# Pooling attention and a token/channel mixer on one core: first batch pooled on TensorE, loads reordered, side work woven at half slots

## The chip, the cores and the metric

The kernel runs on one core of a Trainium2 chip. The metric is device time in microseconds (us), the median over several executions. A profile is one execution with the hardware profiler on. Its engines are PE (TensorE, matmuls; PEld is its load of weights), DVE (VectorE), ACT (ScalarE), POOL (GpSimd) and SP (SyncE, which here only starts transfers).

## The reference

Two parts follow each other. Attention has 8 batches, 8 heads, 576 tokens and 64 columns per head, with keys and values averaged over groups of 8 tokens; the mixer works on 576 x 512 per batch. All inputs and the output are float32.

```python
k_p = k.reshape(B, H, 72, 8, D).mean(axis=3)          # keys, and values likewise
attn = softmax(q @ k_p.T / sqrt(D))                    # 576 x 72 per head
x = (attn @ v_p), heads side by side                   # 576 x 512 per batch
h = relu(x.T @ w_tok1) @ w_tok2                        # over tokens, 256 wide
u = x + h.T
out = u + relu(u @ w_ch1) @ w_ch2                      # over channels, 1536 wide
```

## The kernel before

**Tiling.** The 576 tokens of a batch are split as 64 partitions x 9 rows. Two rows make a chunk of 128 tokens, so a batch has four full chunks and half a one left over; the halves of two batches share a tail chunk. The even rows (0, 2, 4, 6, 8) come first and the odd ones last (`ORDER`, line 41).

**A batch's attention and token mixing** (`batch_steps`, lines 140 to 274) is a list of steps:
- `prepare` (147) pools keys and values by additions (`pool8`, 127: three additions per half of the heads, lines 130, 131 and 133 or 136). Batch 0 is pooled on VectorE, the others on GpSimd (152).
- `kpT` (172) transposes the pooled keys on TensorE into one PSUM buffer `pt`, and VectorE copies them into `kTs` (180). `qT` (184) transposes the queries of a pair of heads into the same `pt` (189), and ScalarE copies them out (191). There is one `pt` buffer (line 57), so each use waits until the one before it was copied out.
- `score` (194) multiplies for two heads, and ScalarE takes the exponential (204).
- `av` (208) is the attention output of one chunk: eight matmuls (214), then VectorE divides (219, 222) into `x`, or `xt` for the half chunk.
- `at` (227), `u` (240) and `uT` (254) are the token mixer, the residual sum and its transpose.

**A unit** (`unit_steps`, 277) is the channel mixer of one batch: 12 groups `g(m)` of four matmuls with w_ch1 (287), each with a Relu on ScalarE or VectorE in turn (290, 292), then for each of four chunks 12 matmuls with w_ch2 in three parts (300), an addition on VectorE (305) and two stores by SP (308). Units 0 to 7 are the batches, unit 8 is the four tail chunks.

**Order of the work.** TensorE and GpSimd run in the order in which the code is written (line 315); VectorE's and ScalarE's order is chosen by the framework's scheduler. The start-up issues all loads on GpSimd's queue: keys, queries and values of batch 0, w_tok1, w_ch1, w_ch2, then batch 1 (lines 316 to 323); w_tok2 goes over SP's queue as float32 (97). At most eight of GpSimd's transfers are under way, and the next waits for the oldest. Batch 0's steps run alone. Then, in unit n, the steps of batch n + 1 are woven between the 24 pieces of the unit, from piece 14 to 26 in unit 0 and from 0 to 22 later, evenly by their number (lines 336 to 343); GpSimd starts the loads of batch n + 2 (333) and pools batch n + 1.

Of the kernel before, what the change touches and what calls it, by code (L numbers as in the profile page):

```python
# [13 lines left out]
POOLE = mybir.EngineType.Pool  # L14


@with_exitstack
def kernel(
# [22 lines left out]
    ORDER = list(range(0, BR, 2)) + list(range(1, BR, 2))  # L41
# [23 lines left out]
    f2 = singles.tile([P, 2, S], FP32)  # L65
# [7 lines left out]
    def load(b):  # L73
        if b >= B:
            return
        kr = raw.tile([SP, H, POOL, D], BF16, name="kr")
        vr = raw.tile([SP, H, POOL, D], BF16, name="vr")
        qb = raw.tile([P, HP * BR * D + D], BF16, name="qb")
        nc.vector.memset(qb[:, HP * BR * D:], 0.0)  # L79
        loaded[b] = (kr, vr, qb)  # L80
        parts = 2 if b == 0 else 1

        def kv(t, src, g):
            n = H // parts
            nc.gpsimd.dma_start(out=t[:, g * n:(g + 1) * n].rearrange("j h i d -> j h (i d)"),  # L85
                                in_=src[b, g * n:(g + 1) * n].rearrange("h (j i) d -> j h (i d)", i=POOL))
        for g in range(parts):
            kv(kr, k, g)
            n = HP // parts
            nc.gpsimd.dma_start(  # L90
                out=qb[:, g * n * BR * D:(g + 1) * n * BR * D].rearrange("p (a e) -> p a e", a=n),
                in_=q[b, 2 * g * n:2 * (g + 1) * n].rearrange("(a l) (p r) d -> (l p) a (r d)", l=2, r=BR))
# [25 lines left out]
    def load_ch():  # L118
# [21 lines left out]
    def batch_steps(b):  # L140
# [6 lines left out]
        def prepare():  # L147
# [24 lines left out]
        def kpT(h0, h1):  # L172
            def go():
# [90 lines left out]
        if first:  # L264
            steps = [kpT(0, HP), qT(0), score(0, 0), score(0, 1), qT(1), score(1, 0), score(1, 1),
                     kpT(HP, H), qT(2), score(2, 0), score(2, 1), qT(3), score(3, 0), score(3, 1)]
        else:
            steps = [kpT(0, H), qT(0), qT(1)]
            for hp in range(HP):
                steps += [score(hp, 0)] + ([qT(hp + 2)] if hp + 2 < HP else []) + [score(hp, 1)]  # L270
        steps += [av(c) for c in range(5)]
        steps += [at(0), at(1), u(0), u(1), uT(0), u(2), uT(1), u(3)]
        steps += ([u(4), uT(2), uT(4)] if par else [uT(2)]) + [uT(3)]
        return prepare, steps, st


    def unit_steps(n, st):
        w = {}

        def g(m):  # L280
            def go():
                if m == 0:
                    w["GT"] = gtp.tile([P, NM, 4 * P], BF16, name="GT")
                uT = uT_tails if n == B else st["uT"]
                ps = ps_one.tile([P, 512], FP32, name="p1")
                for kk in range(4):
                    nc.tensor.matmul(out=ps, lhsT=w_ch1[:, kk, m * P:(m + 1) * P], rhs=uT[:, kk, :],  # L287
                                     start=(kk == 0), stop=(kk == 3))
                if m % 2 == 0:
                    nc.scalar.activation(out=w["GT"][:, m, :], in_=ps, func=AF.Relu)  # L290
                else:
                    nc.vector.tensor_scalar(out=w["GT"][:, m, :], in0=ps, scalar1=0.0, scalar2=None, op0=ALU.max)  # L292
            return go

        def o(c, part):
            def go():
                if part == 0:
                    w["ps"] = ps_one.tile([P, 512], FP32, name="p1")
                for m in range(part * 4, part * 4 + 4):
                    nc.tensor.matmul(out=w["ps"], lhsT=w["GT"][:, m, c * P:(c + 1) * P], rhs=w_ch2[:, m, :],  # L300
                                     start=(m == 0), stop=(m == NM - 1))
                if part < 2:
                    return
                o_sb = outp.tile([P, DM], FP32, name="o")
                nc.vector.tensor_tensor(out=o_sb, in0=w["ps"], in1=(u_tails if n == B else st["u"])[:, c, :], op=ALU.add)
                for half in range(2):
                    b, r = (2 * c + half, ORDER[8]) if n == B else (n, ORDER[2 * c + half])
                    nc.sync.dma_start(out=out[b].rearrange("(p r) n -> p r n", r=BR)[:, r, :],
                                      in_=o_sb[half * BP:(half + 1) * BP, :])
            return go  # L310

# [3 lines left out]
    with tc.manual_schedule(engines={PE, POOLE}):  # L315
# [11 lines left out]
        for s in batches[0][1]:  # L327
            s()
# [45 lines left out]
```

## Time and profile before

| | us |
|---|---|
| median of 3 runs | 333.67 |
| lowest, highest | 332.85, 335.69 |
| profiled execution, its own time | 336.74 |
| span of the profiled execution | 335.0 |
| PE busy | 287.1 (86%) |
| DVE busy | 157.2 (47%) |
| POOL busy | 152.2 (45%) |
| ACT busy | 96.4 (29%) |

The span goes from the first to the last instruction; the profiled execution's own time is 1.74 us longer. Busy time counts an engine's instructions, and for a matmul its modelled end. The unit starts of the profiled execution, from its timeline, are 47.2, 89.6, 124.5, 157.8, 189.9, 223.2, 255.3, 288.5 and 309.3 us.

### The profile page before, as it was taken

The numbers are of one execution on the slowest core, as the hardware profiler recorded it, in microseconds if no ns is written. First come the engines' busy times: TensorE is split into PE (matmuls) and PEld (weight loads), VectorE is DVE, ScalarE is ACT, GpSimd is POOL, SyncE is SP. The second block draws the span as 40 slices with busy tenths as digits, with TensorE's granted clock in tenths as the row PEclk, the third lists the DMA queues.
The fourth block names the chain that finished last, engine by engine and source line by source line (L and its number), as shares of the span: only waits on it lengthen the run. The fifth ranks groups of instructions, "written<-read, shape, count | busy, mean of one in ns | idle before, by whom it ended". The sixth has DMA issues, their size and how long they took to land.

```text
span 335.0 us, 4535 instructions
## 1 busy us (share of the span) xinstructions
PE 287.1 (86%) x1840; PEld 149.9 (45%) x1840; DVE 157.2 (47%) x304; ACT 96.4 (29%) x161; POOL 152.2 (45%) x142
## 2 busy tenths in 40 slices
PE   0026879788699998999899899989998999999994
PEld 0024434453355455544554455445544554444441
DVE  3650554134624653665355526653655266433321
ACT  3026013250056007500750083008302820120300
POOL 7382398089608950994099329999200000000000
PEclk9999999797879999999999999999999999999998
DMA  7999993574327344815291628130022002204114
GB/s 131 184 162 201 204 198 43 101 112 94 58 45 112 62 71 97 135 39 92 73 142 33 104 65 140 38 82 7 0 63 64 2 0 64 65 0 95 33 31 94
DMA packets 26756, 27.95 MB, mean 83 GB/s; under 512 B 4848, under 2 KB 21872, under 8 KB 26736
## 3 DMA queue, kind: packets, MB, share of 16 engines
q0 software_dynamic: 20704, 17.64, 35.3%
q1 hardware_dynamic: 6032, 10.03, 11.9%
q8 instruction: 14, 0.23, 0.3%
q14 instruction: 6, 0.05, 0.0%
HBM read 35.85 MB, written 9.44 MB: 135 GB/s over the span
## 4 chain that ended last, share of the span: by engine, by line
PE 77%; DVE 14%; DMA 4%; ACT 2%; issue 2%; POOL 1%; DVEq 0%; POOLq 0%
DVE x L222 4%; DMA vr<-in_v_dram 4%; PE pt L189 4%; PE pt L260 3%; DVE GT L292 2%; DVE u L251 1%; ACT ex L204 1%; DVE kTs_92 L180 1%; DVE den L219 1%; DVE kTs_91 L180 1%; PE p_504 L300 1%; PE p_644 L300 1%; ACT qT L191 1%; DVE uT L261 1%; PE p_3181 L300 1%
## 5 line engine op out<-in xcount | busy, mean ns | idle before, releaser
L300 PEld LDWEIGHTS <-GT 128*128 128x128 bf16 x432 | 40.2, 98 | 40.6 <-issue 1.1
L287 PEld LDWEIGHTS <-w_ch_86 128*128 128x128 bf16 x432 | 41.3, 99 | 38.1 <-issue 2.4
L90 POOL DMA_DIRECT2D qb<-in_q_dram x9 | 6.9, 770 | 65.9 <-PE pt L189 42.9
L191 ACT COPY qT<-pt 128x640 bf16<-128x640 bf16 x32 | 22.1, 690 | 36.6 <-PE pt L189 36.6
L189 PE MATMUL pt<-ident,qb 128*128 128x128 bf16 x160 | 16.2, 239 | 15.6 <-DVE kTs_91 L180 10.1
L189 PEld LDWEIGHTS <-qb 128*128 128x128 bf16 x160 | 12.5, 108 | 21.7 <-issue 17.4
L214 PEld LDWEIGHTS <-ex 72*128 72x128 bf16 x320 | 14.5, 102 | 13.3 <-DVE x L222 7.5
L176 PE MATMUL pt<-ident,kp 72*128 72x72 bf16 x64 | 4.1, 211 | 15.2 <-DVE kp L133 15.2
L261 DVE COPY uT<-pt 128x512 bf16<-128x512 bf16 x32 | 13.4, 418 | 5.0 <-PE pt L260 5.0
L260 PEld LDWEIGHTS <-u 128*128 128x128 bf16 x128 | 9.6, 97 | 10.8 <-DVE u L251 2.7
L260 PE MATMUL pt<-ident,u 128*128 128x128 bf16 x128 | 12.4, 219 | 2.1 <-DVE uT L261 0.7
L231 PEld LDWEIGHTS <-w_tok_83 128*128 128x128 bf16 x80 | 8.5, 107 | 11.5 <-issue 4.1
L201 PEld LDWEIGHTS <-kTs_91 128*72 128x72 bf16 x64 | 8.1, 129 | 8.9 <-issue 4.3
L176 PEld LDWEIGHTS <-kp 72*128 72x128 bf16 x64 | 3.7, 108 | 17.2 <-DVE kp L133 15.2
L201 PEld LDWEIGHTS <-kTs_92 128*72 128x72 bf16 x64 | 7.2, 115 | 5.9 <-issue 1.0
L250 PEld LDWEIGHTS <-w_tok_84 128*128 128x128 bf16 x64 | 6.1, 99 | 7.2 <-issue 1.4
L85 POOL DMA_DIRECT2D kr<-in_k_dram x9 | 7.6, 842 | 0.9 <-POOLq L358 0.9
L180 DVE COPY kTs_91<-pt 64x576 bf16<-64x576 bf16 (+1 forms) x10 | 3.9, 389 | 8.5 <-PE pt L176 8.4
L85 POOL DMA_DIRECT2D vr<-in_v_dram x9 | 7.4, 819 | 0.4 <-issue 0.4
L79 DVE MEMSET qb<- 128x32 uint32 x8 | 0.7, 85 | 10.5 <-PE pt L189 9.7
L130 POOL TENSOR_TENSOR t_368<-kr 72x1024 f32<-72x1024 bf16 x1 | 2.1, 2113 | 6.0 <-DMA kr<-in_k_dram 6.0
L290 ACT ACTIVATE GT<-p_1495 128x512 bf16<-128x512 f32 x1 | 0.6, 597 | 14.0 <-PE p_1495 L287 14.0
(780 smaller groups left out, 680.0 us busy)
## 6 DMA issues: line engine op xcount, KB each, us to landing
out_dram<-o SPq DMA_DIRECT2D x72, 128.0 KB, 2.4
kr<-in_k_dram POOLq DMA_DIRECT2D x7, 576.0 KB, 8.1
qb<-in_q_dram POOLq DMA_DIRECT2D x7, 576.0 KB, 6.0
vr<-in_v_dram POOLq DMA_DIRECT2D x7, 576.0 KB, 9.7
w_ch_86<-in_moe_w_ch_dram POOLq DMA_DIRECT2D x3, 512.0 KB, 7.2
w_ch_87<-in_moe_w_ch_dram POOLq DMA_DIRECT2D x2, 768.0 KB, 13.8
f_88<-in_moe_w_tok_dram SPq DMA_DIRECT2D x1, 576.0 KB, 4.0
kr<-in_k_dram POOLq DMA_DIRECT2D x2, 288.0 KB, 8.2
```

Source lines behind the costliest of these rows:

```text
L85: nc.gpsimd.dma_start(out=t[:, g * n:(g + 1) * n].rearrange("j h i d -> j h (i d)"), in_=src[b, g * n:(g + 1) * n].rearrange("h (j i) d -> ...
L180: nc.vector.tensor_copy(out=kT[rows, half, h0 * SP:h1 * SP], in_=ps[rows, h0:h1, :].rearrange("p h j -> p (h j)"))
L189: nc.tensor.transpose(out=ps[:, rr].rearrange("m l p -> m (l p)"), in_=st["qb"][:, o:o + P], identity=ident)
L191: nc.scalar.copy(out=st["qT"][:, hp].rearrange("m l (r p) -> m r l p", p=BP), in_=ps)
L201: nc.tensor.matmul(out=ps[0:SP, hl, 0:n], lhsT=kT[:, odd, h * SP:(h + 1) * SP], rhs=st["qT"][:, hp, hl, 0:n], start=True, stop=True)
L214: nc.tensor.matmul(out=ps[:, h // 4, (h % 4) * (D + 1):(h % 4 + 1) * (D + 1)], lhsT=st["ex"][:, h * S + n0:h * S + n0 + P], rhs=st["vp"][: ...
L222: nc.vector.tensor_tensor(out=dst.rearrange("p (a h d) -> p a h d", a=2, d=D), in0=view[:, :, :, 0:D], in1=den[rows, :, :, None].broadcast ...
L231: nc.tensor.matmul(out=ps, lhsT=w_tok1[:, c if c < 4 else 4 + par, m * P:(m + 1) * P], rhs=st["x"][:, c, :] if c < 4 else st["xt"], start= ...
L260: nc.tensor.transpose(out=ps[:, kk, :], in_=src[:, kk * P:(kk + 1) * P], identity=ident)
L261: nc.vector.tensor_copy(out=dst[:, :, o:o + P], in_=ps)
L287: nc.tensor.matmul(out=ps, lhsT=w_ch1[:, kk, m * P:(m + 1) * P], rhs=uT[:, kk, :], start=(kk == 0), stop=(kk == 3))
L300: nc.tensor.matmul(out=w["ps"], lhsT=w["GT"][:, m, c * P:(c + 1) * P], rhs=w_ch2[:, m, :], start=(m == 0), stop=(m == NM - 1))
```

## The change

- **Batch 0 is pooled on TensorE.** `ppool` adds the eight tokens of a group by eight matmuls with the identity into one PSUM bank. Keys are then copied twice, by ScalarE and by VectorE; values once, by VectorE.
- **Loads.** The first two of four head pairs' queries of batch 0 go over SP's queue as float32 and are cast by ScalarE and VectorE; both halves of the keys go first on GpSimd's queue. w_tok2 is cast on its way in, over GpSimd's queue, and VectorE permutes it just ahead of batch 0's outputs. Batch 1 is loaded ahead of w_ch2, which comes in three parts.
- **Odd rows first** (`ORDER`), so that w_tok1 loads in four transfers.
- **Head order by hand**, on VectorE and ScalarE too. In the head VectorE copies the queries and ScalarE half of the keys.
- **Pooling later.** The first half of batches 1 and 2 is pooled on VectorE, the rest on GpSimd. Two small memsets per batch move from GpSimd to VectorE.
- **Weave.** A unit now gives way 48 times: after two matmuls of each g group and of each output chunk. Tables say after which half slot each step of the next batch stands.

In the names below kr, vr and qb are a batch's keys, values and queries as loaded, w_ch_86 and w_ch_87 are w_ch1 and w_ch2, f_88 is w_tok2 as loaded, w_tok_84 is w_tok2 permuted, kp is the pooled keys, pt the transpose buffer, and p_ a PSUM bank.

The first place is GpSimd's queue in the start-up, from w_ch1 to batch 1; before:

```order
L121 DMA w_ch_86<-in_moe_w_ch_dram 128x4x512 x3
L123 DMA w_ch_87<-in_moe_w_ch_dram 128x6x512 x2
L85 DMA kr<-in_k_dram 72x8x512
L90 DMA qb<-in_q_dram 128x4x576
L85 DMA vr<-in_v_dram 72x8x512
```

and after:

```order
L136 DMA w_ch_86<-in_moe_w_ch_dram 128x4x512 x3
L91 DMA kr<-in_k_dram 72x8x512
L95 DMA qb<-in_q_dram 128x4x576
L91 DMA vr<-in_v_dram 72x8x512
L140 DMA w_ch_87<-in_moe_w_ch_dram 128x4x512 x3
```

Batch 1's three transfers now stand ahead of w_ch2.

The second place is VectorE's queue at the first scores of batch 0, with what each instruction waits for; before:

```order
L131 TENSOR_TENSOR t_157<-t_157 72x4x128 [waits DVE_49]
L136 TENSOR_TENSOR vp<-t_153 72x4x64 [waits DVE_49]
L136 TENSOR_TENSOR vp<-t_157 72x4x64 [waits DVE_49]
L169 MEMSET xt 128x256 x2
L180 COPY kTs_91<-pt 64x288 [waits PE_49]
```

and after:

```order
L212 CAST kp<-p_151 72x4x64 [waits Activation_49]
L226 COPY qT<-pt 128x5x2x64 [waits PE_49]
L199 COPY kTs_92<-pt 64x288 [waits Activation_49]
L226 COPY qT<-pt 128x5x2x64 [waits PE_49]
L212 CAST kp<-p_199 72x4x64 [waits Activation_49]
```

The additions that pooled keys and values are gone; copies of pooled keys and of queries stand there, and the copies of pooled and of transposed keys wait for ScalarE's half of the same copy.

The third place is VectorE's queue at batch 0's attention outputs; before:

```order
L79 MEMSET qb 128x32
L219 RECIPROCAL den<-p_242 128x8
L222 TENSOR_TENSOR x<-p_242,den 128x512
L219 RECIPROCAL den<-p_254 128x8
L222 TENSOR_TENSOR x<-p_254,den 128x512
L219 RECIPROCAL den<-p_266 128x8
```

and after:

```order
L129 COPY w_tok_84<-f_88 128x320
L131 COPY w_tok2t<-w_tok_84 128x2x64 x2
L256 RECIPROCAL den<-p_273 128x8
L259 TENSOR_TENSOR x<-p_273,den 128x512
L256 RECIPROCAL den<-p_285 128x8
L259 TENSOR_TENSOR x<-p_285,den 128x512
L256 RECIPROCAL den<-p_297 128x8
L147 TENSOR_TENSOR t_400<-kr 72x1024
L259 TENSOR_TENSOR x<-p_297,den 128x512
L256 RECIPROCAL den<-p_309 128x8
L148 TENSOR_TENSOR t_400<-t_400 72x4x128
L259 TENSOR_TENSOR x<-p_309,den 128x512
```

The permutation of w_tok2 stands ahead of the first output, and batch 1's key additions (t_400) stand between the outputs.

The diff, cut to its core:

```diff
-    ORDER = list(range(0, BR, 2)) + list(range(1, BR, 2))
+    NO = BR - NE
+    ORDER = list(range(1, BR, 2)) + list(range(0, BR, 2))
+    CHUNK = [1, 3, 0, 2]
...
+        if b == 0:
+            for a in range(2):
+                nc.sync.dma_start(out=qf[:, a:a + 1, :], in_=q_in(a, a + 1))
+            kv(kr, k, 0, HP)
+            kv(kr, k, HP, H)
+            make_identity(nc, ident)
+            q_cast(2, HP)
+            kv(vr, v, 0, HP)
+            kv(vr, v, HP, H)
+            nc.scalar.copy(out=qb[:, 0:BR * D], in_=qf[:, 0, :])
+            nc.vector.tensor_copy(out=qb[:, BR * D:2 * BR * D], in_=qf[:, 1, :])
+        else:
+            kv(kr, k, 0, H)
+            q_cast(0, HP)
+            kv(vr, v, 0, H)
 
     def load_tok():
-        nc.sync.dma_start(out=f2, in_=moe_w_tok2.rearrange("(c p) n -> p c n", p=P))
+        nc.gpsimd.dma_start(out=f2, in_=moe_w_tok2.rearrange("(c p) n -> p c n", p=P))
...
+    def permute_tok2():
         src = f2.rearrange("t m (p r) -> t m r p", r=BR)
         dst = w_tok2.rearrange("t m (r p) -> t m r p", p=BP)
         for m in range(2):
-            nc.scalar.copy(out=dst[:, m, 0:NE], in_=src[:, m, 0:BR:2, :])
-            nc.vector.tensor_copy(out=dst[:, m, NE:BR], in_=src[:, m, 1:BR:2, :])
+            nc.vector.tensor_copy(out=dst[:, m, 0:NO], in_=src[:, m, 1:BR:2, :])
+            nc.vector.tensor_copy(out=dst[:, m, NO:BR], in_=src[:, m, 0:BR:2, :])
...
+            if not first:
+                engs = [nc.vector if b < 3 else nc.gpsimd, nc.gpsimd]
+                for g in range(2):
+                    hs = slice(g * HP, (g + 1) * HP)
+                    pool8(engs[g], kr, hs, kp[:, hs], True)
...
+                    copy = nc.scalar.copy if first and half == 0 else nc.vector.tensor_copy
+                    copy(out=kT[rows, half, h0 * SP:h1 * SP], in_=ps[rows, h0:h1, :].rearrange("p h j -> p (h j)"))
+        def ppool(t, g):
+            def go():
+                ps = ps_one.tile([P, 512], FP32, name="p1")
+                hs = slice(g * HP, (g + 1) * HP)
+                for i in range(POOL):
+                    nc.tensor.matmul(out=ps[0:SP, 0:HP * D], lhsT=ident[0:SP, 0:SP], rhs=st[t][:, hs, i, :],
+                                     start=(i == 0), stop=(i == POOL - 1))
+                view = ps[0:SP, 0:HP * D].rearrange("j (h d) -> j h d", d=D)
+                if t == "kr":
+                    nc.scalar.copy(out=st["kp"][:, hs, 0, :], in_=view)
+                    nc.vector.tensor_copy(out=st["kp"][:, hs, 1, :], in_=view)
+                else:
+                    nc.vector.tensor_copy(out=st["vp"][:, hs, 0:D], in_=view)
...
-                nc.scalar.copy(out=st["qT"][:, hp].rearrange("m l (r p) -> m r l p", p=BP), in_=ps)
+                dst = st["qT"][:, hp].rearrange("m l (r p) -> m r l p", p=BP)
+                if first:
+                    nc.vector.tensor_copy(out=dst, in_=ps)
+                else:
+                    nc.scalar.copy(out=dst, in_=ps)
...
+                nc.tensor.matmul(out=ps, lhsT=w_ch1[:, kk, m * P:(m + 1) * P], rhs=uT[:, kk, :],
+                                 start=(kk == 0), stop=(kk == 3))
+                if kk == 1:
+                    yield
...
+                if m % 2 == 1 and m < NM - 1:
+                    yield
...
+    HEAD = """kpool0 q0 kpT0 o0 e0 q1 o1 e1 kpool1 q2 kpT1 o2 e2 q3 o3 e3 vpool0 vpool1 av0 av1 av2 av3 av4
+              at0 at1 u0 u1 t0 u2 t1 u3 t2 t3"""
...
+    LATER = {0: "kpT", 2: "q0", 4: "q1", 5: "o0", 6: "q2", 7: "e0", 9: "o1", 10: "q3", 11: "e1", 13: "o2", 15: "e2",
...
+        with tc.manual_schedule(engines={DVE, ACT}):
+            load(0)
...
+            load_tok()
+            load_ch1()
+            load(1)
+            load_ch2()
+            batches[0][0]()
+            for s in HEAD.split():
+                if s == "av0":
+                    permute_tok2()
+                batches[0][1][s]()
         for n in range(B + 1):
...
+            for i, _ in enumerate(unit_steps(n, batches[n][2] if n < B else None)):
+                for s in at.get(i, "").split():
+                    if (n + 1) % 2 or s not in ("u4", "t4"):
+                        side[s]()
```

In `HEAD` and the tables o and e are a pair's scores of odd and even rows, q, t and u stand for `qT`, `uT` and `u`. In unit 0 the table `FIRST` begins with `kpT0` at half slot 14 and ends with `t3 t4` at 47; in `LATER` av0 stands at 22, at0 at 32, u0 at 36, and t4, which only odd batches have, at 47.

## Rows read from the trace of the kernel before

**Rows 1.** Units' stretches: length; PE, PEld, DVE, ACT, POOL busy; clock, DMA share, GB/s.
```profile
47.20:57.73 10.53, 10.53 (x49) 4.79 (x49) 3.46 (x5) 3.58 (x6) 10.14 (x9) 1.00 0.66 94
57.73:89.61 31.88, 25.50 (x174) 13.57 (x173) 14.21 (x30) 7.78 (x13) 20.03 (x18) 0.89 0.50 89
89.61:124.49 34.88, 33.58 (x215) 17.79 (x215) 15.98 (x31) 11.25 (x19) 19.95 (x17) 0.90 0.45 72
124.49:157.82 33.33, 32.03 (x223) 17.02 (x222) 17.82 (x35) 11.26 (x19) 19.97 (x17) 1.00 0.50 90
157.82:189.91 32.09, 30.79 (x215) 16.52 (x214) 16.67 (x32) 11.26 (x19) 19.96 (x17) 1.00 0.48 84
```

**Rows 2.** Waits of TensorE, 15 to 89, then 89 to 289 us: total, times, longest.
```profile
PE pt L176 <- DVE kp L133: 15.2, 1, 15.2
...
PE pt L189 <- DVE kTs_91 L180: 6.7, 2, 6.0
...
PE pt L189 <- DVE kTs_91 L180: 3.3, 3, 1.1
...
PE pt L189 <- DVE kTs_92 L180: 3.3, 3, 1.1
```

**Rows 3.** The same view in stretches of 2 us.
```profile
36.00:38.00 2.00, 1.78 (x18) 1.06 (x16) 1.93 (x5) 0.00 (x0) 0.00 (x0) 1.00 1.24 208
...
60.00:62.00 2.00, 0.58 (x10) 0.34 (x9) 1.51 (x3) 0.00 (x0) 0.00 (x0) 1.00 0.93 153
62.00:64.00 2.00, 1.20 (x11) 0.97 (x12) 0.00 (x0) 0.73 (x2) 0.00 (x0) 0.70 1.00 217
64.00:66.00 2.00, 2.00 (x7) 0.83 (x6) 0.00 (x0) 0.66 (x1) 0.00 (x0) 0.50 0.05 16
```

**Rows 4.** Timeline of the start-up, its chain: start, length, engine, line.
```profile
8.52 1.22 DVE L130 TENSOR_TENSOR t_145<-kr 72x1024 f32<-72x1024 bf16 x1 [2.61 <-DMA kr<-in_k_dram]
...
24.05 0.74 PE L189 MATMUL pt<-ident,qb 128*128 128x128 bf16 x5
...
24.94 0.69 ACT L191 COPY qT<-pt 128x640 bf16<-128x640 bf16 x1
...
26.41 0.70 ACT L204 ACTIVATE ex<-p_197 72x640 bf16<-72x640 f32 x1 [0.78 <-PE p_197 L201]
```

**Rows 5.** The same timeline, TensorE in at(0) and at(1), and GpSimd.
```profile
37.01 1.90 PE L231 MATMUL p_302<-x,w_tok_83 128*128 128x512 bf16 x4
...
39.05 2.11 POOL L130 TENSOR_TENSOR t_368<-kr 72x1024 f32<-72x1024 bf16 x1 [6.03 <-DMA kr<-in_k_dram]
...
39.12 1.91 PE L231 MATMUL p_309<-x,w_tok_83 128*128 128x512 bf16 x4
...
40.83 0.63 PE L231 MATMUL p_309<-xt,w_tok_83 128*128 128x512 bf16 x1
```

**Rows 6.** The same timeline, VectorE alone.
```profile
4.73 0.79 DVE L114 CAST w_tok_84<-f_88 128x256 bf16<-128x256 f32 x2 [1.68 <-DMA f_88<-in_moe_w_tok_dram]
...
5.55 0.32 DVE L116 COPY w_tok2t<-w_tok_84 128x128 bf16<-128x128 bf16 x2
...
13.29 0.68 DVE L131 TENSOR_TENSOR t_145<-t_145 72x512 f32<-72x512 f32 x1
...
14.49 0.68 DVE L133 TENSOR_TENSOR kp<-t_145 72x512 bf16<-72x512 f32 x1
...
20.07 0.42 DVE L136 TENSOR_TENSOR vp<-t_157 72x256 bf16<-72x256 f32 x1
...
27.07 0.62 DVE L180 COPY kTs_91<-pt 64x288 bf16<-64x288 bf16 x2 [5.56 <-PE pt L176]
...
36.67 0.69 DVE L222 TENSOR_TENSOR x<-p_278,den 128x512 bf16<-128x512 f32 x1
...
37.50 0.68 DVE L222 TENSOR_TENSOR xt<-p_290,den 64x512 bf16<-64x512 f32 x1
...
43.89 0.41 DVE L261 COPY uT<-pt 128x512 bf16<-128x512 bf16 x1
```

More of the change, by code (lines that the diff above doesn't have):

```diff
@@ L80, in load @@
         loaded[b] = (kr, vr, qb)
[L81 to L92, printed above, removed]
@@ L108, in load_tok @@
+        for half in range(2):
+            rows = slice(half * BP, (half + 1) * BP)
             nc.gpsimd.dma_start(out=w_tok1[rows, 4 + half, :], in_=w[:, ORDER[8], :])
-        nc.vector.memset(w_tok2t, 0.0)
+    def permute_tok2():
         src = f2.rearrange("t m (p r) -> t m r p", r=BR)
@@ L262, in uT @@
             return go
[L264 to L272, printed above, removed]
@@ L273, in batch_steps @@
-        steps += ([u(4), uT(2), uT(4)] if par else [uT(2)]) + [uT(3)]
-        return prepare, steps, st
-    def unit_steps(n, st):
[L278 to L310, printed above, removed]
-        return [g(m) for m in range(NM)] + [o(c, part) for c in range(4) for part in range(3)]
@@ L315 @@
[L315 to L328 removed]
+        name = {f"kpT{g}": kpT(g * HP, (g + 1) * HP) for g in range(2)}
+        name["kpT"] = kpT(0, H)
@@ new lines, in batch_steps @@
+        for g in range(2):
+            name[f"kpool{g}"], name[f"vpool{g}"] = ppool("kr", g), ppool("vr", g)
+        for hp in range(HP):
+            name[f"q{hp}"], name[f"o{hp}"], name[f"e{hp}"] = qT(hp), score(hp, 1), score(hp, 0)
+        for c in range(5):
+            name[f"av{c}"], name[f"u{c}"], name[f"t{c}"] = av(c), u(c), uT(c)
+        name["at0"], name["at1"] = at(0), at(1)
+        return prepare, name, st
+    def unit_steps(n, st):
+        GT = gtp.tile([P, NM, 4 * P], BF16, name="GT")
+        uT = uT_tails if n == B else st["uT"]
+        u_all = u_tails if n == B else st["u"]
+        for m in range(NM):
+            ps = ps_one.tile([P, 512], FP32, name="p1")
+            for kk in range(4):
+                nc.tensor.matmul(out=ps, lhsT=w_ch1[:, kk, m * P:(m + 1) * P], rhs=uT[:, kk, :],
+                                 start=(kk == 0), stop=(kk == 3))
+                if kk == 1:
+                    yield
+            if m % 2 == 0:
+                nc.scalar.activation(out=GT[:, m, :], in_=ps, func=AF.Relu)
+            else:
+                nc.vector.tensor_scalar(out=GT[:, m, :], in0=ps, scalar1=0.0, scalar2=None, op0=ALU.max)
+            yield
+        for c in range(4):
+            ps = ps_one.tile([P, 512], FP32, name="p1")
+            for m in range(NM):
+                nc.tensor.matmul(out=ps, lhsT=GT[:, m, c * P:(c + 1) * P], rhs=w_ch2[:, m, :],
+                                 start=(m == 0), stop=(m == NM - 1))
+                if m % 2 == 1 and m < NM - 1:
+                    yield
+            o_sb = outp.tile([P, DM], FP32, name="o")
+            nc.vector.tensor_tensor(out=o_sb, in0=ps, in1=u_all[:, c, :], op=ALU.add)
+            for half in range(2):
+                b, r = (2 * c + half, ORDER[8]) if n == B else (n, ORDER[2 * c + half])
+                nc.sync.dma_start(out=out[b].rearrange("(p r) n -> p r n", r=BR)[:, r, :],
+                                  in_=o_sb[half * BP:(half + 1) * BP, :])
+            yield
```

88 lines of the change are left out of this document (40 added, 48 removed).

## The prediction

> **What bounds the kernel now.** I read the share of busy time first, then the span cut at the starts of the stages, then the waits of TensorE, its clock in short stretches, and last the timeline of the start-up. TensorE is the bound in most of the span: in units 2 and 3 it is busy 32.03 of 33.33 us and 30.79 of 32.09 us, so a steady unit loses 1.30 us [rows 1]. The time to be had is elsewhere. Up to 47.2 us no unit has begun: TensorE first waits 15.2 us for VectorE's pooling of the keys, then 6.0 us for the copy into kTs, which stands behind the pooling of the values on VectorE [rows 2]. Unit 0 then takes 10.53 + 31.88 = 42.4 us, although its work is that of unit 2 (32.03 us): TensorE is idle 6.4 us of it, and the granted clock is 0.89 in its second part [rows 1]. In short stretches that is 0.50 in 64 to 66 us, the 1.2 GHz level, after a stretch at 60 to 62 us in which TensorE worked 0.58 of 2 us [rows 3]. Unit 1 takes 34.88 us at a clock of 0.90 where unit 3, with the same work, takes 32.09 [rows 1].
>
> **Head.** Edits: pooling of batch 0 by identity matmuls, half the queries over SP, VectorE's and ScalarE's order by hand. I follow the new chain in us of the span.
>
> The first half of the keys lands when it does now, as the same bytes go ahead of it on SP's queue (0.59 MB, w_tok2 or these queries): 8.5 [rows 4]. Each pooling is eight matmuls of 256 columns; four of 512 columns go in 39.12 to 40.83 us [rows 5], 0.43 each and so at the 1.2 GHz level, which makes 0.21 for 256 columns and 1.7 a pooling: 10.2. Its two copies out run one after the other, since the order makes VectorE's wait for ScalarE's. A copy of 72 x 256 is no row out of PSUM; VectorE's 72 x 256 out of SBUF took 0.42 [rows 6], and I take 0.4 each (bounds 0.3 and 0.7): 11.3. The copy of the queries, now on VectorE, must free the one transpose buffer before the keys' transposes: uT of 128 x 512 took 0.41 there [rows 6], so 0.5 for 640 columns against ScalarE's 0.69 [rows 4]: 11.9. Transposes 0.45, and two copies into kTs, also in series, 0.85 (two took 0.62 [rows 6], plus a hand-over): 13.2. Scores of a head pair (1152 columns at that rate) 0.96, transposes of the next queries 0.74 [rows 4], copy with hand-overs 0.7, scores 0.96: 16.6. The second half repeats this with its pooling in front (4.6 before the scores, 3.35 for them): 24.5. The two poolings of the values 3.4 and their copy 0.55: 28.5. Then, by the order, VectorE permutes w_tok2 before it may touch the first attention output: two of 128 x 256 took 0.79, two of 320 would take 0.96, and the two small copies 0.32 [rows 6]: 30.5.
>
> There the gain is mostly given back. Five outputs at 0.83 from one to the next [rows 6] are 4.2, and between them stand three additions for batch 1 (1.22 [rows 4], 0.68, 0.68 [rows 6]), 2.6 in all: the last output xt is ready at 37.3, where it now ends at 38.2 [rows 6]. One matmul of at0 and five of at1 follow (now the last begins at 40.83 [rows 5]); unit 0 begins 1.2 us earlier, at 46.0. VectorE stalls if batch 1's keys are not there at about 32.4. They land at 39.05 now [rows 5]; w_ch2, 1.5 MB that no longer goes before them, is 7.6 us at the 208 GB/s of [rows 3], so 31.5: just in time. If they came as late as now, xt would end near 44, 5.9 us later than before. Were the paired copies parallel and the value poolings at the high clock, it would be 2 us better.
>
> [...]
>
> One cost is unknown. The matmuls of at0 and at1 now run as one dense stretch of 4.2 us from 37.0 [rows 5]; it is behind this stretch that unit 0 begins at the high clock. With xt late that stretch is broken, and unit 0 may begin at 1.2 GHz. That costs between nothing and the 1.6 us of one slow spell (0.30 x 2 + 0.50 x 2 us lost in 62 to 66 us [rows 3]); I take 0.9. Head in all: -0.3, bounds -3.2 and +5.9.
>
> **Unit 0 (batch 1 woven in).** The attention of batch 1 now begins at 60 us, behind 13 matmul groups; it will begin after 14 half slots (6 us), since its keys are pooled in halves by VectorE and GpSimd from 31.5 on and not after 39.05. Its pieces lie over 34 half slots of 0.43 us. I walked the list through: waits of 0.5 (queries behind kTs), 0.2, 1.3 (ScalarE has four copies of 0.69, four exps of 0.70 [rows 4], and six narrower exps and Relus of about 0.6 by their width, 9.2 us, in some 8.8 us of slots), 1.9 (VectorE has five outputs, two output additions and 2.3 us of pooling of batch 2 (1.22, 0.68 and 0.42 [rows 4, 6]) where at0 waits for xt) and 1.1 at the end: 5.0 at most, and I take 4.0 as some overlap. 32.5 of work (42.4 less 6.4 idle and 3.5 of clock) + 4.0 = 36.5: -5.9. Bounds: -9.9 if idle time and clock loss all go, -2 if the waits double. VectorE would stall here too if batch 2's keys were late. w_ch2 is last in the queue now; it has until about 58 us.
>
> **Unit 1.** 34.88 becomes 30.8 of work + 1.2 of waits, with no slow spell: -2.9 (bounds 0 and -3.8).
>
> **Units 2 to 6.** The waits are those of the first query transposes for kTs, 6.6 us in all [rows 2]. Two half slots now lie between (0.86): about 0.5 us is left per unit. But behind a batch with a tail (units 3 and 5) the tail's transposes stand last, and the next keys' transposes wait for that buffer behind an output addition: 1.2 there. So 3 x 0.8 + 2 x 0.1 = -2.6 (bounds -6.5, all of it, and +3, 0.6 worse each). Units 7 and 8 have no side work: 0. GpSimd's pooling from batch 3 on is as before.
>
> **Sum.** -0.3 - 5.9 - 2.9 - 2.6 = -11.7 us. The profiled execution took 336.74 us, 335.0 of them the span; it would be 325.0. The median of the runs shown is 333.67, 3.1 below the profiled one, so I forecast 322.0.
>
> **Rivals.**
> 1. The head gains too: copies that I put in series overlap, the value poolings run at 2.4 GHz, unit 0 begins at the high clock, and its waits are near 2 us. Head -3, unit 0 -8, the rest as above: -16.5, 317. For it: ScalarE's part is small; against it: VectorE's permutation and batch 1's additions stand in series before xt, whatever TensorE does. Chance 0.25.
> 2. Late keys: VectorE waits for batch 1's keys some 3 us and for batch 2's 1 to 2 us, with at0 queued behind the outputs each time. Head +3, unit 0 -2.5, unit 1 -1.5: about -3.6, 330. For it: VectorE takes its work in order, and TensorE needs the outputs that stand behind; against it: the queue's gap at the start closes. Chance 0.14.
> 3. The clock: where the side work is spread thin with a wait at each piece, TensorE drops to 1.2 GHz once in every woven unit, and twice in unit 0 as now. A spell costs 1.6 us, eight cost 12.8; with a head 3.3 us worse (its upper half) the sum is -11.7 + 12.8 + 3.3 = +4.4, 338. Alone it decides from the eighth spell on (11.7 / 1.6). Against it: in units 2 and 3 the clock is 1.00 with 1.1 us waits in them [rows 1, 2]. Chance 0.04.
> 4. No effect: the head's chain ends with xt as now and unit 0 stays bound by the order of its evictions: within 1%. Chance 0.07.
>
> **Numbers.** Forecast 322.0, chance 0.5. The range goes from 314 (rival 1 with its bounds) to 330 (rival 2); what lies outside has about 0.15. A change of 1%, 3.3 us, is about what a measurement can tell from none. Faster by more 0.89, within it 0.07, slower 0.04.
>
> **What would show it.** The first matmul near 8.5 us; xt near 37; unit 0's first matmul near 46, and whether its first groups take 0.86 or 1.7 us; unit 0 of 36 to 37 us; the first addition for batch 1 on VectorE with no DMA wait ahead of it; units 2, 4 and 6 about 0.8 us shorter than now, 3 and 5 the same. A first unit that begins after 48, a clock under 0.97 in a later unit, or a VectorE wait of over 2 us for kr would make the forecast wrong.

## The result and the profile after

The changed kernel takes 323.18 us (median of 4 runs, 321.43 to 327.12), against 334.26 for the kernel before (4 runs beside it). Of the four, 327.12 is a slow run, and the ratio to the kernel before, 0.9651 with a 95% interval of 0.9561 to 0.9741, is taken from the other three (321.43, 321.55, 324.80): faster by 3.5%. The profiled execution took 321.55 us, with a span of 319.7, where the one before took 336.74 with 335.0. So the two profiles differ by 15 us and the medians by 11; the stages below are read from the profiles.

First the span cut at the starts of the units, in the changed kernel (columns as in [rows 1]), and as its last row units 0 to 7 together. Behind it stands that last row for the kernel before.

```profile
46.06:84.32 38.26, 32.72 (x218) 16.89 (x222) 26.42 (x47) 11.51 (x19) 12.40 (x9) 1.00 0.58 97
84.32:115.19 30.87, 30.27 (x212) 16.43 (x215) 16.67 (x34) 11.21 (x19) 19.80 (x15) 1.00 0.42 70
115.19:147.06 31.87, 31.42 (x219) 17.03 (x222) 18.06 (x37) 11.21 (x19) 19.78 (x15) 1.00 0.54 95
147.06:178.31 31.25, 30.34 (x215) 16.41 (x216) 17.26 (x35) 11.21 (x19) 19.79 (x15) 1.00 0.48 86
...
46.06:293.94 247.88, 238.22 (x1595) 126.66 (x1627) 138.19 (x262) 82.36 (x139) 108.10 (x80) 1.00 0.39 71
```

```profile
47.20:309.10 261.90, 247.71 (x1627) 129.57 (x1627) 127.03 (x241) 82.27 (x139) 126.69 (x107) 0.97 0.38 69
```

The head gave 1.1 us. Unit 0 fell from 42.4 to 38.3, unit 1 from 34.9 to 30.9, units 2 and 3 from 33.3 and 32.1 to 31.9 and 31.3 [rows 1]. The granted clock is 1.00 in all of them, so the spells at 0.50 of [rows 3] are gone. A pause of TensorE does not bring such a spell by itself: from 72 to 74 us it worked 0.42 of 2 us, less than at 60 us in [rows 3], and the clock stayed at 1.00. What does bring one stays open.

```profile
72.00:74.00 2.00, 0.42 (x2) 0.14 (x2) 1.82 (x6) 0.00 (x0) 1.92 (x3) 1.00 0.11 40
74.00:76.00 2.00, 1.95 (x9) 0.93 (x10) 0.20 (x3) 0.60 (x1) 0.54 (x1) 1.00 0.30 29
```

In unit 0 TensorE is still idle 38.26 - 32.72 = 5.5 us, and VectorE is busy 26.4 us, far more than in any later unit.

What TensorE waits for now (total, times, longest), answering to [rows 2]:

```profile
PE p_151 L207 <- DMA kr<-in_k_dram: 6.8, 1, 6.8
PE p_321 L251 <- DVE x L259: 3.0, 1, 3.0
PE p_297 L251 <- DVE x L259: 2.2, 1, 2.2
...
PE p_671 L268 <- DVE x L259: 1.2, 1, 1.2
PE p_671 L268 <- DVE xt L259: 1.2, 1, 1.2
```

The waits of 15.2 and 6.0 us for VectorE's pooling and for kTs are gone. In their place stand waits for x and xt, the attention outputs. The timeline shows what VectorE does then (start, length, engine, line); L147, L148 and L150 are additions of the pooling.

```profile
6.85 1.86 PE L207 MATMUL p_151<-kr,ident 72*72 72x256 bf16 x8 [6.85 <-DMA kr<-in_k_dram]
...
29.97 2.12 POOL L147 TENSOR_TENSOR t_404<-kr 72x1024 f32<-72x1024 bf16 x1
...
30.21 2.98 DVE L147 TENSOR_TENSOR t_400<-kr 72x1024 f32<-72x1024 bf16 x1
...
32.17 2.13 POOL L148 TENSOR_TENSOR t_404<-t_404 72x512 f32<-72x512 f32 x1
...
33.11 0.68 DVE L259 TENSOR_TENSOR x<-p_297,den 128x512 bf16<-128x512 f32 x1
...
33.83 1.03 DVE L148 TENSOR_TENSOR t_400<-t_400 72x512 f32<-72x512 f32 x1
...
33.84 0.62 PE L251 MATMUL p_321<-vp,ex 72*128 72x65 bf16 x8 [2.99 <-DVE x L259]
...
36.45 0.67 DVE L259 TENSOR_TENSOR xt<-p_321,den 64x512 bf16<-64x512 f32 x1
...
46.06 1.02 PE L321 MATMUL p_422<-uT,w_ch_86 128*128 128x512 bf16 x4 [0.52 <-DVE uT L298]
...
69.11 2.11 POOL L147 TENSOR_TENSOR t_786<-vr 72x1024 f32<-72x1024 bf16 x1
...
69.22 2.55 DVE L148 TENSOR_TENSOR t_782<-t_782 72x512 f32<-72x512 f32 x1
...
72.42 0.38 PE L268 MATMUL p_671<-x,w_tok_83 128*128 128x512 bf16 x1 [1.24 <-DVE x L259]
```

The first addition for batch 1 took 2.98 us on VectorE, where the same shape took 1.22 in [rows 4], and GpSimd's second took 2.13 where its later ones take 1.26. Each time the other engine was adding too. VectorE's ended at 30.21 + 2.98 = 33.19, which is 1.10 behind the end of GpSimd's (29.97 + 2.12 = 32.09). At 69 us it is the same: VectorE's ended at 71.77, 0.55 behind GpSimd's 71.22. That looks as if the second to begin stands still until the first is through.

### The profile page after: what moved, and what is told of

The parts are those of the page before. It is cut to its first block, busy times and chain, and to the rows that moved or that the text cites. A ratio compares the mean times of both kernels' runs of the same rounds, so it can differ in the third digit from the quotient of the medians.

```text
span 319.7 us, 4561 instructions
## 1 busy us (share of the span) xinstructions
PE 285.1 (89%) x1837; PEld 153.0 (48%) x1872; DVE 168.5 (53%) x329; ACT 94.9 (30%) x160; POOL 136.0 (43%) x115
## 4 chain that ended last, share of the span: by engine, by line
PE 72%; DMA 11%; DVE 7%; POOL 5%; issue 2%; ACT 1%; POOLq 0%
DMA kr<-in_k_dram 8%; DMA f_88<-in_moe_w_tok_dram 3%; PE pt L222 3%; PE pt L297 2%; DVE o L338 2%; DVE kTs_92 L199 1%; PE p_1453 L333 1%; DVE kTs_93 L199 1%; PE p_1312 L333 1%; PE p_2140 L333 1%; PE p_1006 L333 1%; PE p_3216 L333 1%; PE p_1826 L333 1%; PE p_2185 L333 1%; PE p_2769 L333 1%
## 5 line engine op out<-in xcount | busy, mean ns | idle before, releaser
L333 PEld LDWEIGHTS <-GT 128*128 128x128 bf16 x432 | 39.0, 97 | 38.4 <-issue 1.8
L321 PEld LDWEIGHTS <-w_ch_86 128*128 128x128 bf16 x432 | 40.1, 98 | 30.6 <-issue 0.6
L95 POOL DMA_DIRECT2D qb<-in_q_dram x8 | 6.2, 771 | 72.2 <-PE pt L222 70.5
L251 PEld LDWEIGHTS <-ex 72*128 72x128 bf16 x320 | 16.1, 102 | 15.5 <-DVE x L259 6.9
L228 ACT COPY qT<-pt 128x640 bf16<-128x640 bf16 x28 | 19.3, 690 | 7.2 <-PE pt L222 7.2
L222 PE MATMUL pt<-ident,qb 128*128 128x128 bf16 x160 | 15.3, 230 | 1.8 <-DVE kTs_92 L199 0.7
L268 PEld LDWEIGHTS <-w_tok_83 128*128 128x128 bf16 x80 | 8.2, 103 | 13.1 <-issue 4.9
L287 PEld LDWEIGHTS <-w_tok_84 128*128 128x128 bf16 x64 | 6.4, 101 | 8.4 <-issue 1.9
L207 PEld LDWEIGHTS <-ident 72*72 72x72 bf16 x32 | 5.8, 180 | 7.8 <-POOL ident masks.py:199 3.5
L207 PE MATMUL p_151<-kr,ident 72*72 72x256 bf16 x8 | 1.9, 411 | 6.8 <-DMA kr<-in_k_dram 6.8
```

Of the source, the lines that this page charges most:

```text
L207: nc.tensor.matmul(out=ps[0:SP, 0:HP * D], lhsT=ident[0:SP, 0:SP], rhs=st[t][:, hs, i, :], start=(i == 0), stop=(i == POOL - 1))
L222: nc.tensor.transpose(out=ps[:, rr].rearrange("m l p -> m (l p)"), in_=st["qb"][:, o:o + P], identity=ident)
L228: nc.scalar.copy(out=dst, in_=ps)
L251: nc.tensor.matmul(out=ps[:, h // 4, (h % 4) * (D + 1):(h % 4 + 1) * (D + 1)], lhsT=st["ex"][:, h * S + n0:h * S + n0 + P], rhs=st["vp"][: ...
L268: nc.tensor.matmul(out=ps, lhsT=w_tok1[:, CHUNK[c] if c < 4 else 4 + par, m * P:(m + 1) * P], rhs=st["x"][:, c, :] if c < 4 else st["xt"], ...
L333: nc.tensor.matmul(out=ps, lhsT=GT[:, m, c * P:(c + 1) * P], rhs=w_ch2[:, m, :], start=(m == 0), stop=(m == NM - 1))
```

## The experiments

Theory A was that these additions side by side are what keeps the gain small. The first four runs try it, and the load order and the weave beside it.

**All pooling of batches 1 and 2 on GpSimd.**

```
- engs = [nc.vector if b < 3 else nc.gpsimd, nc.gpsimd]
+ engs = [nc.gpsimd, nc.gpsimd]
```

> Batches 1 and 2 pooled on GpSimd alone; all else as in the changed kernel. Theory A (the additions for batches 1 and 2 on VectorE stand in the way, and they are slow because GpSimd adds at the same time): without them the outputs of batch 0 follow one another at 0.84 us, xt ends near 32.6 instead of 37.1 us, unit 0 begins near 41.5 instead of 46.1, and the 2.4 us in which at(0) of batch 1 waits for its outputs go: a span near 312, a median near 315.5. Rival B (TensorE waits for GpSimd instead, which now pools 18.5 us of batch 1 from 30 us on): kpT of batch 1 waits, unit 0 gets longer by 2 us or more, and the median stays within 2 us of the changed kernel's 323.

317.4 us (315.06 to 317.59), ratio to before 0.9498 (0.9462 to 0.9534): theory A's side, though 1.9 us more than its 315.5, with unit 0 at 42.98 and not 41.5. Head, then units 0 to 7:

```profile
0.00:42.98 42.98, 25.44 (x151) 16.83 (x152) 18.00 (x53) 9.00 (x15) 28.17 (x35) 1.00 1.16 187
42.98:287.50 244.52, 239.64 (x1627) 126.80 (x1627) 129.88 (x253) 82.36 (x139) 122.46 (x93) 1.00 0.42 75
```

The head is 3.1 us shorter than in the changed kernel and units 0 to 7 are 3.4 us shorter, although batch 0's keys came 1.3 us later (8.15 against 6.85). GpSimd needs some 18 us for a batch, and no wait of TensorE's names it.

**The same on VectorE alone.** `engs = [nc.vector if b < 3 else nc.gpsimd] * 2`.

> Both halves of batches 1 and 2 are pooled on VectorE, so GpSimd adds nothing while VectorE does. Read is the length of the first addition for batch 1 between batch 0's outputs, at the same place as in the changed kernel (2.98 us there, and 1.03 twice). Theory A (VectorE's float32 additions out of SBUF are slowed by GpSimd's at the same time): 1.22, 0.68 and 0.68. Rival B (the loads that write SBUF at 200 GB/s slow it, GpSimd has no part): about 2.98 and 1.03 again.

A single run: 316.93 us. VectorE's additions between the outputs:

```profile
31.47 1.17 DVE L147 TENSOR_TENSOR t<-kr 72x1024 f32<-72x1024 bf16 x1
...
33.27 0.64 DVE L148 TENSOR_TENSOR t<-t 72x512 f32<-72x512 f32 x1
```

They stand in the same place, while transfers run as before (205 GB/s from 29 to 36 us in both), and take 1.17 and 0.64 us. So the 2.98 and 1.03 came from GpSimd's additions, not from the transfers. Either engine alone is better than both.

**w_ch2 loaded ahead of batch 1 again.** `load_ch2()` moved in front of `load(1)`.

> The changed kernel with w_ch2 loaded ahead of batch 1 again. The scheduler then puts VectorE's first addition for batch 1 behind the Relu of at(1) and not between batch 0's outputs. Theory A (VectorE takes its work in order and stops at keys that have not landed): the keys of batch 1 land near 37.6 us, VectorE waits about 1 to 2 us for them with the residual sums queued behind, and again for the values near 45; unit 0 begins at 44 to 46 us and is 1 to 3 us longer: -1 to +3 us. Rival B (the load order decides the start-up): unit 0 begins 7 us later and the time is 6 us or more longer.

321.02 us (319.36 to 322.96), ratio 0.9611 (0.9559 to 0.9664), no slower than the whole change. Neither forecast had this: theory A had unit 0 at 44 to 46 us. With the keys late, the scheduler's order lets VectorE finish the outputs first, and unit 0 begins at 42.97. VectorE and GpSimd then begin almost together:

```profile
37.30 1.21 DVE L147 TENSOR_TENSOR t<-kr 72x1024 f32<-72x1024 bf16 x1
```

```profile
37.33 3.16 POOL L147 TENSOR_TENSOR t<-kr 72x1024 f32<-72x1024 bf16 x1 [7.72 <-DMA kr<-in_k_dram]
```

Here VectorE is first by 0.03 us and loses nothing, and GpSimd takes 3.16 instead of 2.12: the stall changes sides with the order of the starts.

**The old weave in the changed kernel.** The pieces of the next batch stand at whole slots again, in the old order.

```
- side, at = batches[n + 1][1], FIRST if n == 0 else LATER
+ side, at = batches[n + 1][1], whole(n + 1)
```

> The changed kernel with the weave of before: whole pieces, from piece 14 in unit 0, the list of before. Theory A (the weave alone is what shortens the units): units 2 to 6 go back to 33.3 and 32.1 us (+6.0 together), unit 1 to 32.1 or more (+1.2 to +4.0), unit 0 becomes 2 to 4 us longer: 9 to 14 us more than the changed kernel, so nothing left against the kernel before but the head's 1.1. Rival B (odd rows first, pooling on VectorE and the cast loads shorten the units): less than 3 us more than the changed kernel.

341.81 us (340.28 to 342.03), ratio 1.0222 (1.0183 to 1.0261): slower than before, and 18.6 us slower than the whole change, more than theory A had expected of the weave. Unit 0 begins at 49.23. VectorE's additions lie between the outputs again, beside GpSimd's, the first of the two last copies of the permutation (L131) takes 2.55 us and the second 0.18, and at 80 us TensorE is back at 1.2 GHz, as in [rows 3]:

```profile
29.71 2.65 DVE L131 COPY w_tok2t<-w_tok 128x128 bf16<-128x128 bf16 x2
...
34.07 1.88 DVE L147 TENSOR_TENSOR t<-kr 72x1024 f32<-72x1024 bf16 x1
...
36.59 1.89 DVE L148 TENSOR_TENSOR t<-t 72x512 f32<-72x512 f32 x1
...
77.15 1.95 DVE L148 TENSOR_TENSOR t<-t 72x512 f32<-72x512 f32 x1
```

```profile
30.07 2.13 POOL L147 TENSOR_TENSOR t<-kr 72x1024 f32<-72x1024 bf16 x1
...
33.61 1.26 POOL L150 TENSOR_TENSOR kp<-t 72x512 bf16<-72x512 f32 x1
35.40 2.52 POOL L147 TENSOR_TENSOR t<-vr 72x1024 f32<-72x1024 bf16 x1 [0.53 <-DMA vr<-in_v_dram]
```

```profile
76.00:80.00 4.00, 1.00 (x21) 0.75 (x21) 4.00 (x7) 0.00 (x0) 3.84 (x3) 0.72 0.91 189
80.00:84.00 4.00, 4.00 (x16) 1.50 (x14) 2.10 (x6) 0.00 (x0) 1.80 (x3) 0.50 0.28 24
```

The ends fit the pattern: VectorE's 35.95 is 1.08 behind GpSimd's 34.87, and its 38.48 is 0.56 behind 37.92; the first copy ended at 29.71 + 2.55 = 32.26, as GpSimd's addition did (32.20). So two things, weave and stall, were mixed in this run, and the next takes them apart.

**The old weave with all pooling on GpSimd.** The edit of the run before and the first one, together.

> Edit: the changed kernel with the pieces at whole slots, as in e2_whole_slots, and all additions of batches 1 and 2 on GpSimd. Theory (the loss of e2_whole_slots against the kernel before came from VectorE's additions beside GpSimd's, which the scheduler put between the head's outputs and those of unit 0): unit 0 begins near 43 us as in e1_pool_gpsimd instead of 49.2, and the units are those of the kernel before, 42 and 35 us with spells at 1.2 GHz and then 32 to 33; about 329 to 331 us. Rival (the new load order or the order of the halves does not suit the old weave, whoever pools): 337 us or more.

332.21 us (330.78 to 336.41), ratio 0.9925 (0.9888 to 0.9962), a little above the theory's 329 to 331. The 9.6 us below the run before are what VectorE's additions beside GpSimd's cost under the old weave. Units 0 to 7 take 258.7 us against 244.5 with the new weave. The head was to begin unit 0 at 43 and did at 45.4, through one copy of the permutation that VectorE began at 29.39:

```profile
29.28 2.94 DVE L131 COPY w_tok2t<-w_tok 128x128 bf16<-128x128 bf16 x2
```

```profile
29.17 0.84 POOL L91 DMA_DIRECT2D vr<-in_v_dram  x1 [2.60 <-DMA kr<-in_k_dram]
30.03 2.13 POOL L147 TENSOR_TENSOR t<-kr 72x1024 f32<-72x1024 bf16 x1
```

The first of the two copies took 0.20; the second ended at 32.22, as GpSimd's addition did (32.16). It stood from 29.39 on, while GpSimd issued a transfer (29.17 to 30.01) and then added. A copy has one source, so it is not only additions of two operands that stand.

**The weave alone, in the kernel before.** Generator and tables of the change, all else as before.

> Edit: the kernel before with the weave at half slots alone (generator and position tables of the change; head, loads, order of the token positions, engines of the pooling and the scheduling of VectorE and ScalarE as before). Theory (the weave carries the gain from unit 1 on, and VectorE's additions beside GpSimd's take from unit 0 what it gives): unit 0 begins at 47.2 as before, it takes 35 to 38 us instead of 42.4, units 1 to 6 take together 10 us less; 317 to 321 us, so no slower than the whole change. Rival (the weave needs the order by hand and the earlier keys of batch 1): unit 0 gains nothing, units 1 to 6 gain the forecast 5.5 us; 328 us or more.

318.58 us (318.3 to 318.79), ratio 0.951 (0.9456 to 0.9563). One part alone does better than the whole change.

```profile
0.00:46.50 46.50, 17.53 (x117) 10.88 (x119) 22.50 (x52) 10.58 (x16) 24.52 (x36) 1.00 1.15 180
46.50:290.80 244.30, 237.55 (x1594) 126.79 (x1626) 129.55 (x243) 82.44 (x139) 127.64 (x107) 1.00 0.41 74
```

```profile
54.08 0.44 PE L189 MATMUL pt<-ident,qb 128*128 128x128 bf16 x5 [0.38 <-DVE kTs L180]
60.50 0.65 PE L201 MATMUL p<-qT,kTs 128*72 128x256 bf16 x4 [0.35 <-ACT qT L191]
62.73 0.38 PE L201 MATMUL p<-qT,kTs 128*72 128x256 bf16 x2 [0.44 <-ACT qT L191]
79.23 0.38 PE L260 MATMUL pt<-ident,u 128*128 128x128 bf16 x4 [0.53 <-DVE uT L261]
81.16 0.38 PE L260 MATMUL pt<-ident,u_tails 128*128 128x128 bf16 x4 [0.65 <-DVE uT L261]
```

These five are the waits of TensorE that the timeline shows inside unit 0, which ends at 81.38; they come to 2.35 us, and none is for x or xt. The head is that of before, within 0.7 us; the units are as short as with GpSimd alone in the changed kernel. So the gain from unit 0 on is the weave's, 261.9 to 244.3 us, and the changed kernel (247.9) gives 3.6 us of it back. Of the 17.6 us some 7 are slow clock that is gone (0.11 of 31.88 and 0.10 of 34.88 us [rows 1], an estimate), and TensorE's idle time falls from 14.2 to 6.8 us. Finer pieces and new positions came together here; no run has one without the other, so which of them counts is not shown.

**Batch 0 pooled by VectorE's additions again**, at the same places; the rest as changed.

```
- for i in range(POOL): nc.tensor.matmul(... ident ...)
+ pool8(nc.vector, st[t], hs, ...)
```

> Edit: of the change, only the pooling of batch 0 by identity matmuls is undone; VectorE adds at the same places of its order (2.58 us for half the keys, 2.32 for half the values). Theory (the pooling by TensorE saves little, as its eight matmuls of 1.7 us at 1.2 GHz and the copies out of 0.8 us take as long as VectorE's additions): batch 0's values are pooled by about 26 us as now, unit 0 begins within 1 us of 46.06, 322 to 324.5 us. Rival (VectorE's 9.8 us of additions push the copies behind them, as in the kernel before, where the copy into kTs stood behind them for 6.0 us): unit 0 begins 3 us later or more, 326 us or more.

322.43 us (322.2 to 322.95), ratio 0.9627 (0.9581 to 0.9672). Unit 0 begins at 46.0. Pooling by identity matmuls, the first edit that the change names, is worth nothing here that can be measured. The stall is there again, and again VectorE (33.13) ends 1.09 us behind GpSimd (32.04):

```profile
29.91 2.13 POOL L147 TENSOR_TENSOR t<-kr 72x1024 f32<-72x1024 bf16 x1
```

```profile
30.28 2.85 DVE L147 TENSOR_TENSOR t<-kr 72x1024 f32<-72x1024 bf16 x1
```

**All pooling on GpSimd, and w_tok2 permuted ahead of the values' pooling**, where VectorE stands idle: `if s == "vpool0":` instead of `"av0"`.

> Edit: all additions of batches 1 and 2 on GpSimd (as in e1_pool_gpsimd) and, besides, the permutation of w_tok2 moved ahead of the pooling of batch 0's values in VectorE's order. In e1_pool_gpsimd VectorE stands idle from 22.5 to 25.5 us and permutes from 27.5 to 29.7, with TensorE's attention outputs waiting 2.23 us behind it. Theory (the permutation is on the path to xt): the first output's reciprocal comes at about 27.6 instead of 29.7, xt 2 us earlier, unit 0 at 41 instead of 42.98; about 315.4 us. Rival (TensorE runs at 1.2 GHz up to the first unit, and its matmuls, not VectorE, set the pace of the outputs; a break in its work may also cost a slow spell): xt gains under 0.7 us, 317 us or more.

313.12 us (312.84 to 313.57), ratio 0.9348 (0.9303 to 0.9392), the best of the study, 2.3 us under what the theory gave. The permutation now runs from 22.58 to 24.88, and xt comes at 31.82 instead of 33.29.

```profile
0.00:41.50 41.50, 25.20 (x149) 16.84 (x151) 18.10 (x53) 9.01 (x15) 28.14 (x35) 1.00 1.13 189
41.50:286.00 244.50, 237.75 (x1595) 126.77 (x1627) 129.88 (x253) 82.44 (x139) 122.50 (x93) 1.00 0.42 76
```

The profiled spans differ from those with the late permutation by 1.5 us, all of it in the head; the medians by 4.3 us. The profiled execution with the late permutation was its fastest, 315.06 against 317.06 to 317.59 of the other four, so the profiles do not show the rest.

**The two named edits taken out of this best version**, one at a time: the old load order, then VectorE's additions for batch 0.

> Edit: e5_early_permute with w_ch2 loaded ahead of batch 1 again, as in the kernel before. Theory (the new load order has no worth of its own: nothing on VectorE waits for batch 1's keys any more, and GpSimd has pooled a half of them by some 48 us if they come at 39): unit 0 begins at 41.5 as in e5_early_permute, its first key transposes at half slot 14 (47.5 us) wait 1 to 2 us; 313 to 315.5 us. Rival (GpSimd, 18.5 us for a batch, is on the path of unit 0, so that 7 to 9 us later keys come through): unit 0 longer by 5 us or more, 318 us or more.

> Edit: e5_early_permute with batch 0 pooled by VectorE's additions at the same places (as in e6_head_pool_dve). Theory (TensorE's pooling is worth nothing here either: its 1.9 us for a half at 1.2 GHz and two copies stand on TensorE's own path, VectorE's 2.58 and 2.32 us beside TensorE's scores): unit 0 begins within 1 us of 41.5, 312 to 314.5 us. Rival (with the permutation early VectorE is full, and the pooling of the values ends later by the difference of 4.6 us of additions and 0.8 us of copies): unit 0 begins 2.5 us later or more, 315.5 us or more.

313.69 us (ratio 0.9397, 0.9348 to 0.9446) and 313.86 us (ratio 0.9393, 0.9346 to 0.9440). Neither differs from 313.12 by what can be measured. Units 0 to 7 take 244.4 and 244.5 us. With the old loads the first key transposes, at half slot 14, waited for nothing and the query transposes behind them 0.38 us for kTs, as in the weave alone: GpSimd has pooled that half of the keys by 43.3 us.

**Is it a stop, or a shared rate?** GpSimd's first addition of each pooling, in the changed kernel, as two of half the size.

> Edit: the changed kernel with the first addition of each of GpSimd's poolings (72 x 1024 out, 2.12 us) issued as two of 72 x 512. Theory (of two additions out of SBUF on VectorE and GpSimd, the one that begins second stands still until the other's instruction ends): in the changed kernel VectorE's first addition for batch 1 began at 30.21, GpSimd's of 29.97 ended at 32.09, and 32.09 + 1.1 = 33.19 is where VectorE's ended, after 2.98 us. With halves GpSimd's first ends at about 31.05, so VectorE's takes 0.85 + 1.1 = 1.9 to 2.1 us, and GpSimd's second half is the one that stands (2.0 us or more instead of 1.06). Rival (both run at once and share the rate of the memory): GpSimd is as busy as before while VectorE adds, so VectorE's addition takes 2.7 us or more, and both halves about 1.1 us.

A single run, 320.85 us.

```profile
31.34 2.32 DVE L150 TENSOR_TENSOR t<-kr 72x1024 f32<-72x1024 bf16 x1
```

```profile
30.31 2.26 POOL L150 TENSOR_TENSOR t<-kr 72x512 f32<-72x512 bf16 x2
32.65 2.14 POOL L151 TENSOR_TENSOR t<-t 72x512 f32<-72x512 f32 x1
```

Neither forecast came true as written. VectorE began 1.1 us later than I had assumed, at the end of the first half, and the second half went ahead of it undisturbed (1.15 us each). But VectorE ended at 33.66, again 1.09 behind GpSimd's 32.57. In four runs with four starts the end of VectorE's first addition lies 1.08 to 1.10 us behind GpSimd's, which a shared rate would not give, and GpSimd's own, where it began first and was not halved, took 2.12 and 2.13 us as it does alone. A stop explains all of it. Which of the two gets in between two instructions of the other is open.

The Trainium skill (SBUF — State Buffer, Who interferes with whom) says just this: VectorE's second pair of memory ports is GpSimd's only one, it is an exclusive lock, and an addition with two operands in SBUF, or a copy in one of VectorE's two-port modes, contends with a GpSimd addition. The runs agree, with 2.98 against 1.17 us and the copy of 2.83 against 0.20. By that page VectorE's additions from PSUM (L259, 0.68 us) do not contend, and they don't: 0.68 at 33.11 us in the changed kernel, with GpSimd's addition of 32.17 running to 34.30.

## Why the prediction was right, and where it was not

The time was right: 322.0 forecast, 323.18 measured. In part that is luck: the sum was -11.7 us, and between the two profiled executions the stages gave 15.3. I took the median to lie 3.1 us below the profiled execution, as before; for the changed kernel it lies 1.6 above it, and the two errors cancel. Several terms were wrong too.

**Head, -0.3 forecast, -1.1 measured: errors that cancel, and one charge not paid.** The first pooling began at 6.85 us in the profiled execution instead of 8.5. In the experiments with the same first loads, keys came at 7.9 to 9.0, around the forecast, so this execution was early by luck. Little of it was left at the end: the last experiment, with keys at 7.98, began unit 0 at 46.3. My chain then held: scores, copies in series and value poolings of 1.7 us at the 1.2 GHz level (22.21 to 23.92 us, so 0.21 for 256 columns, though the granted clock reads 1.00 there; in unit 0 512 columns take 0.22) are in the timeline much as worked out. Of the outputs behind it the term of the three additions for batch 1, "2.6 in all", failed: they took 2.98 + 1.03 + 1.03 = 5.0. The permutation took 2.2 us for its four large copies instead of 0.79 + 0.96 = 1.75: 0.38 for 256 columns, as I had, but 0.72 for 320. So the last output came at 37.1 instead of 37.3. The 0.9 us for a slow start of unit 0 was not paid: its first group took 0.9 us and not 1.7, although the dense stretch was broken by 1.0 us before xt.

**Unit 0, -5.9 forecast, -4.2 measured.** TensorE is idle 5.5 us where I took 4.0. The term that failed is the 1.9 us where at0 waits for xt behind "2.3 us of pooling of batch 2": its three additions took 1.35 + 2.55 + 0.53 = 4.4, and TensorE waited 0.50 for an output and 1.24 and 1.16 at at0, 2.9 in all. In the weave alone, with all of it on GpSimd, none of the three waits is there, and unit 0 takes 81.38 - 46.51 = 34.9 us.

**Unit 1, -2.9 forecast, -4.0 measured; units 2 to 6, -2.6 forecast, -6.0 measured.** The mechanism was right, the size off. I had left 0.5 us of waiting for kTs per unit and 1.2 for the tail's buffer; the waits are 0.2 and 0.5 to 0.7. The rest, some 0.5 us a unit, is less busy time of TensorE (30.34 against 30.79 in unit 3, from 215 recorded matmuls each), which I had taken as fixed. Why it fell I cannot say.

**The rivals.** Late keys (rival 2) did not come: the first addition has no wait for a transfer ahead of it, and batch 2's keys were there at 54.1. The clock (rival 3) was 1.00 in every unit. Rival 1, a head and unit 0 that gain too, has the time of the kernel as soon as the two engines no longer add side by side, 317 against 317.4, but not its terms. There the poolings of the values still take 1.7 us each, at the 1.2 GHz level, and the span falls by 4.2 in the head, 7.5 in unit 0, 4.0 in unit 1 and 6.0 in units 2 to 6, 21.7 in all, where rival 1 had 3, 8, 2.9 and 2.6, 16.5 in all. That the times agree is chance.

**What I missed altogether** is the split of the pooling between the engines. I priced VectorE's additions from [rows 4, 6], where GpSimd adds nothing, and put them beside GpSimd's. No row of before shows both at once, so it was an unknown cost that I did not bound. I also gave the head's edits the credit for unit 0's earlier start of batch 1; the weave alone, with keys landing at 39, does the same.

So of the change, the weave alone carries the time from 334.7 to 318.6 us; the rest, put on it, costs 4.6 us net by the medians, 3.0 by the profiled spans (319.7 against 316.7). The identity matmuls and the load order are worth nothing that can be measured. Pooling on two engines at once costs 5.8 us by the medians (323.18 against 317.4) and 6.4 by the profiled spans, and the place of the permutation between 1.5 (spans) and 4.3 (medians). The best version is 5.5 us below the weave alone, so something in the rest does gain: what of the order by hand, the queries over SP and the odd rows first does it was not taken apart.

## What to carry to other kernels

A duration read where the other engine is idle is not its duration beside it: when work is split between VectorE and GpSimd, look whether both read SBUF at once, and give each its own time or leave the work to one. Spreading filler work in pieces of half a matmul group, at places chosen so that each wait has work in front of it, was worth more here (16.1 us) than all that the rest of the change gave even in its best version (5.5 us). Before crediting a change of many parts, run its largest part alone.

## What the runs showed that I had not expected

- An instruction of VectorE can stand for the whole of one of GpSimd's: 2.98 us against 1.17, and a copy of 128 x 128 2.83 against 0.20. It goes the other way too: 3.16 against 2.12 on GpSimd, where VectorE was first by 0.03 us.
- Beside a transfer's issue by GpSimd a copy can take longer as well. With all pooling on VectorE the two copies of 128 x 128 took 0.54 and 0.47 us and ended at 29.81 and 29.85, with an issue from 28.98 to 29.82; in the old weave with all pooling on GpSimd the first of them, begun 0.11 us into an issue, took 0.20. An addition was not held: at 17.39 us in the kernel before it took 1.21, with issues running from 16.44 to 18.69.
- A strided copy of bf16 on VectorE took 0.38 us for 256 columns and 0.72 for 320, in every run but for two copies of 256 columns beside such an issue (0.53 with batch 0 pooled by VectorE, 0.50 with the old loads in the best version); I have no explanation for the step.
- Pooling eight tokens by identity matmuls at the 1.2 GHz level (1.7 us and two copies) is no faster than VectorE's three additions (2.58 us), as both stand in the same chain.
